# Transposing q by whole-array passes of the transpose mode for every unit of a fused attention and two-MLP kernel

## The chip, the cores and the metric

The kernel runs on one core of a Trainium2 chip. Its engines work side by side, each through an instruction list of its own, in order: PE (TensorE, matrix products, with a weight load ahead of each product), DVE (VectorE), ACT (ScalarE), POOL (GpSimd) and SP (SyncE, which here issues every DMA). The metric is the device time of one execution in microseconds; less is better.

## The reference, cut to what matters

```python
# q, k, v: (4, 8, 576, 64) float32, phi: (4, 8, 576, 32) float32
a = softmax(phi, axis=2)                        # over the 576 tokens
k_m = einsum('bhsm,bhsd->bhmd', a, k)           # 32 memory rows per head
v_m = einsum('bhsm,bhsd->bhmd', a, v)
attn = softmax(q @ k_m.T / 8)                   # over the 32 memories
x = (attn @ v_m).transpose(0, 2, 1, 3).reshape(2304, 512)
h = max(x @ w1, x @ w2, x @ w3)                 # 512 -> 768, weights in float64
x = h @ w_out                                   # 768 -> 512
g = softplus(x @ w_in)                          # 512 -> 2048
out = g @ w_out2                                # 2048 -> 512
```

## The kernel before, in words

**Units.** The attention is cut into eight units u = 0..7; a unit is one batch entry and four of its eight heads (u = 2 * batch + group). Units 0 to 3 are the first pair of batch entries, 4 to 7 the second pair. For a unit, phi, k and v are loaded, the softmax over tokens is made, and the compressed keys and values (32 memories of 4 heads stacked on 128 partitions, tile kvd) are transposed by small products with a 0/1 constant (L389 for values, and for the keys of units 0 to 3; L408 with another constant, `pick`, for the keys of units 4 to 7). att_q brings q to qT (head dimension on partitions, tokens along the row), att_sc multiplies it by the keys (L462 for units 0 to 3, L465 for 4 to 7), and the softmax over 32 memories follows as a chain over engines: att_sm0 (DVE: L474 transposes in 32x32 blocks, L477 takes the maximum), att_sm1 (POOL or DVE subtracts, L484; ACT takes the exponential, L485), att_sm2 (DVE sums, L491 to L493; POOL or DVE multiplies, L495), att_fin (DVE transposes back, L501; ACT rounds to the matrix format as ah, L506; al is what the rounding lost).

**q in two ways.** For units 0 to 3 (the set QPE), one DMA per unit brings 512 tokens of four heads, 4 neighbouring tokens of a head to a partition (1,024 bytes in a run), and a second one the last 64 tokens. PE multiplies each 128x64 block with the identity (L443, 16 blocks; L446, 4 blocks of 64 tokens), which leaves a head's transpose on half of the columns, and ACT's cast (L213) puts the tokens back into order with a strided write. For units 4 to 7 one DMA brings whole rows of 18 tokens (4,608 bytes), and DVE's transpose of 32x32 blocks (L452) makes all of qT in one instruction.

**MLP stages.** Values are multiplied into the weights first: u_mm (L565, and u_mr with L583 to L585 for the second pair) gives u = v w, in two parts uh and ul, and m1 multiplies u by attn (L611: ah by uh, al by uh, ah by ul, 18 matmuls for one block). m1out (L653 to L655) is the product with w_out, y0_split and L853, L885 are the second MLP. The float64 weights come as pairs of int32 (tile wraw) and are turned to float by ACT (L246), DVE and POOL. Four stages follow one another before the second MLP: phase_a(0) is m1 of the first pair, together with the keys and values of units 4 to 7; phase_o(0) is m1out of the first pair, and at slots from a table (`scs`) it takes up att_q, att_sc and the softmax of units 4 to 7; phase_a(1) is m1 of the second pair, which needs the ah of units 4 and 5, then that of 6 and 7; phase_o(1) ends the first MLP.

**What sets the order.** A list (PLAN) gives the program order of the first stages. From the program order a scheduler makes each engine's own order, and rotating buffers hold it back: products of units 4 to 7 share two PSUM tiles (pst), the others six (psm). q of units 4 to 7 has one buffer (tag qr), so that load_q(u + 1) is called after att_sc(u). SP issues all loads in its order, and each issue waits for the landing of the eighth one before it.

Of the kernel before, what the change touches and what calls it, by code (L numbers as in the profile page):

```python
# [117 lines left out]
C = {  # L118
    'load5': 5,
    'att': [[9, 9, 10, 11, 11], [10, 12, 12, 13, 13], [13, 13, 15, 15, 15], [15, 18, 19, 21, 21]],  # L120
    'wo': [[4, 5, 5], [6, 7, 7], [11, 11, 14], [11, 13, 17], [21, 22, 24], [23, 23, 23]],
    'scs': [[4, 4, 4, 4, 5, 6], [5, 5, 5, 6, 6, 7], [6, 6, 6, 7, 10, 10], [8, 11, 12, 13, 14, 18]],
    's1': ['pool', 'pool', 'pool', 'dve'],
    's2': ['dve', 'pool', 'pool', 'dve'],
    'al': ['pool', 'pool', 'pool', 'dve'],
    'u6': 7,
# [3 lines left out]
    'hl': ['dve'] + ['pool'] * 16 + ['dve'],  # L130
    'us0': 1,
    'us1': 0,
    'qpe': (0, 1, 2, 3),
}

@with_exitstack
def fused_kernel(ctx: ExitStack, tc: tile.TileContext, q, k, v, phi, w1, w2, w3, w_out, m_in, m_out, out):
# [7 lines left out]
    nc = tc.nc  # L145
    B, H, S, D = q.shape
# [3 lines left out]
    P = 128  # L150
# [28 lines left out]
    t_p = pool(a2_s, "a2", side="left")  # L179
# [18 lines left out]
    nc.vector.memset(onesq, 1.0)  # L198
    y1 = {}

    pick = const.tile([P, 4, P], F32, name="pick")
    pick2 = const.tile([P, 2, P], F32, name="pick2")
    nc.gpsimd.memset(pick, 0.0)
    nc.gpsimd.memset(pick2, 0.0)
    for h in range(4):
        a = slice(32 * h, 32 * h + 32)
        nc.vector.tensor_copy(pick[a, h, a], ident[a, a])
# [58 lines left out]
    units = [(b, g) for b in range(B) for g in range(NG)]  # L266
    U = defaultdict(dict)
    attn, vT = {}, {}
    QPE = C["qpe"]
    CK = {}  # L270

    def new_vT(pp):
# [34 lines left out]

    def load_q(u):
        b, g = units[u]
        if u in QPE:  # L310
            hs = slice(4 * g, 4 * g + 4)
            x = y1a_p.tile([P, 4, R4, D], F32, tag=f"ya{u}", name="qn")
            xr = wo_p.tile([SREM, 4, D], F32, tag=f"wol{2 + u}", name="qnr")
            dma(out=x.rearrange("p h r d -> p h (r d)"),
                in_=q[b, hs, 0:R4 * P, :].rearrange("h (p r) d -> p h (r d)", r=R4))
            dma(out=xr, in_=q[b, hs, R4 * P:S, :].rearrange("h p d -> p h d"))
            U[u]["qr"] = (x, xr)
            return
        if u < 4:
            qr = y1a_p.tile([P, NJB, 2, 32], F32, tag=f"ya{u}", name="qr")  # L320
        else:
            qr = t_p.tile([P, NJB, 2, 32], F32, tag="qr", name="qr")
        dma(out=qr.rearrange("p j a c -> p (j a c)"),
                          in_=q[b, 4 * g:4 * g + 4].rearrange("h (p j) d -> (h p) (j d)", j=NJB))
        U[u]["qr"] = qr

    def att_max(u):
        d = U[u]
# [52 lines left out]
    def att_tr(u, i):  # L381

        d = U[u]
        b, g = units[u]
        bl = b % 2
        st, kvd = d.pop(("xp", i)), d.pop(("kvd", i))
        if i or u in QPE:
            for s in range(2):
                nc.tensor.matmul(st[64 * s:64 * s + 64, P:2 * P], kvd, pick2[:, s], start=True, stop=True)  # L389
            if not i:  # L390
                kT = t_p.tile([P, 2, 64], F32, tag="kT", name="kT", bufs=4)
                nc.scalar.activation(out=kT, in_=st[:, P:2 * P].rearrange("p (a c) -> p a c", a=2), func=AF.Copy)
                d["kT"] = kT
                return
            CK["v", b, g] = 1
            sv = st[:, P:2 * P].rearrange("p (a c) -> p a c", a=2)
            if b < 2:
                nc.scalar.activation(out=vT[0][:, 2 * g:2 * g + 2, bl], in_=sv, func=AF.Copy)
                return
            vh, vl = vT[1]  # L400
            s0, sp = 4 * g + bl, 3 - 2 * bl
            nc.scalar.activation(out=vh[:, s0:s0 + sp + 1:sp, :], in_=sv, func=AF.Copy)
            nc.vector.tensor_tensor(out=vl[:, s0:s0 + sp + 1:sp, :], in0=sv, in1=vh[:, s0:s0 + sp + 1:sp, :],
                                    op=ALU.subtract)
            return
        for hf in range(2):
            for h in range(4):
                nc.tensor.matmul(st[32 * h:32 * h + 32, (1 + hf) * P:(2 + hf) * P], kvd[:, 32 * hf:32 * hf + 32],  # L408
                                 pick[:, h], start=True, stop=True)
        kT = t_p.tile([P, 2, 2, 64], F32, tag="kT", name="kT", bufs=4)  # L410
        sk = st[:, P:3 * P].rearrange("p (a s c) -> p a s c", a=2, s=2)
        if bl == 0:
            nc.scalar.activation(out=kT, in_=sk, func=AF.Copy)
        else:
            for s in range(2):
                nc.scalar.activation(out=kT[:, :, s], in_=sk[:, :, 1 - s], func=AF.Copy)
# [6 lines left out]
    def att_trs(u):  # L423
        att_tr(u, 1)
        att_tr(u, 0)

    def att_q(u, remeng="act"):
        d = U[u]
        qr = d.pop("qr")
        if u == 1:  # L430
            qT = h_p.tile([P, 2, S], F32, tag="h0", name="qT")
        elif u == 3:
            qT = y1a_p.tile([P, 2, S], F32, tag="ya0", name="qT")
        else:
            qT = t_p.tile([P, 2, S], F32, tag="qT", name="qT")
        if u in QPE:
            x, xr = qr
            rem = psm()
            for s in range(2):
                qp = psm()  # L440
                for r in range(R4):
                    for a in range(2):
                        nc.tensor.matmul(qp[64 * a:64 * a + 64, r * P:(r + 1) * P], x[:, 2 * s + a, r], ident,  # L443
                                         start=True, stop=True)
                for a in range(2):
                    nc.tensor.matmul(rem[64 * a:64 * a + 64, s * 64:s * 64 + 64], xr[:, 2 * s + a],  # L446
                                     ident[0:SREM, 0:SREM], start=True, stop=True)
                cast("act", qT[:, s, 0:R4 * P].rearrange("x (p r) -> x r p", r=R4), qp.rearrange("x (r p) -> x r p", r=R4))
            cast(remeng, qT[:, :, R4 * P:S], rem[:, 0:P].rearrange("p (s c) -> p s c", s=2))
            d["qT"] = qT  # L450
            return
        nc.vector.transpose(out=qT.rearrange("x a (p j) -> x a j p", j=NJB), in_=qr.rearrange("p j a c -> p a j c"))  # L452
        d["qT"] = qT

    def att_sc(u):
        d = U[u]
        kT, qT = d.pop("kT"), d.pop("qT")
        d["sc"] = []
        for c in range(2):
# [261 lines left out]
    def conv(i, p):  # L721
# [24 lines left out]
    for n in range(4):  # L746
        u = 4 + n
# [15 lines left out]
    for n in range(4):  # L763
        u = 4 + n
# [187 lines left out]
```

## Time and profile before

| what | value |
|---|---|
| median of 3 runs | 742.25 us (740.18 to 743.65) |
| the profiled execution | 739.94 us |
| its span in the trace | 738.1 us |
| its mean granted TensorE clock | 0.993 of full speed |
| PE busy | 703.9 us (95%) in 4808 instructions |
| DVE busy | 413.2 us (56%) |
| ACT busy | 297.6 us (40%) |
| POOL busy | 251.2 us (34%) |

The profiled execution lies 1.84 us above its span and 2.31 us below the median. PE is busy for 95% of the span, but not evenly: what it loses lies in the first 100 us and around 190 to 225 us, so that those stages are read by themselves.

### The profile page before, as it was taken

To read this page: it belongs to the slowest core of one execution; us is meant where nothing else is said; L and a number is where in the kernel's file an instruction comes from. 1 tells how busy PE (TensorE), PEld (TensorE's weight loads), DVE (VectorE), ACT (ScalarE), POOL (GpSimd) and SP (SyncE) were. 2 spreads that over 40 slices of the span, in tenths; PEclk is the share of its full clock that TensorE was granted. 3 is DMA by queue.
4 is the path that set the end of the run, shared out by engine and by line. 5 is a ranking of instruction groups with operands and counts; after the bars stand their busy time and mean duration, and the time that the engine had idled before them with its cause. 6 is when DMAs were issued, how large, how long until landed. Compare 5 with 4: busy or idle time off the path is not lost. (4 is left out here: it accounts for less than half of the span.)

```text
span 738.1 us, 12457 instructions
## 1 busy us (share of the span) xinstructions
PE 703.9 (95%) x4808; PEld 620.8 (84%) x4808; DVE 413.2 (56%) x788; ACT 297.6 (40%) x618; POOL 251.2 (34%) x240
## 2 busy tenths in 40 slices
PE   4979899999979999989999999999999999999997
PEld 3646777899869999978989889899888989889895
DVE  4479785426969974683332585333794335333342
ACT  2456464324567743653333453223442224222221
POOL 1012323114775414752222453222642224322221
PEclk9999999999999999999999999999999999999999
DMA  8997790201234201450000132000230000011112
GB/s 249 271 306 232 237 281 34 85 4 43 65 110 126 94 1 31 142 148 24 1 0 1 29 114 87 1 1 0 86 118 26 1 1 1 0 44 44 43 46 84
DMA packets 55195, 59.26 MB, mean 80 GB/s; under 512 B 10080, under 2 KB 49504, under 8 KB 55136
## 3 DMA queue, kind: packets, MB, share of 16 engines
q1 hardware_dynamic: 55136, 58.47, 26.4%
q8 instruction: 38, 0.62, 0.4%
q14 instruction: 21, 0.17, 0.1%
HBM read 53.74 MB, written 4.72 MB: 79 GB/s over the span
## 5 line engine op out<-in xcount | busy, mean ns | idle before, releaser
L221 POOL TENSOR_TENSOR gl<-m,gh 128x384 fp32r<-128x384 f32 x96 | 100.5, 1048 | 253.5 <-ACT gh L213 236.5
L859 DVE TENSOR_SCALAR e<-pst 128x384 int32<-128x384 int32 x96 | 53.1, 554 | 134.1 <-PE pst L853 134.0
L861 ACT ACTIVATE L<-e 128x384 f32<-128x384 f32 x96 | 50.3, 524 | 184.1 <-DVE e L859 184.1
L885 PE MATMUL acc<-oh,gh 128*128 128x512 f32 x288 | 113.7, 395 | 0.4 <-ACT gh L213 0.4
L885 PE MATMUL acc<-ol,gh 128*128 128x512 f32 x288 | 113.4, 394 | 0.0
L853 PE MATMUL pst<-yb,ih 128*128 128x384 f32 x384 | 102.1, 336 | 0.0
L611 PE MATMUL psm<-ah,uh 128*128 128x288 f32 x288 | 87.5, 308 | 3.7 <-ACT ya L213 2.5
L611 PE MATMUL psm<-ah,ul 128*128 128x288 f32 x288 | 85.5, 299 | 0.3 <-DVE ul L570 0.3
L611 PE MATMUL psm<-al,uh 128*128 128x288 f32 x288 | 85.7, 298 | 0.0
L863 DVE SCALAR_TENSOR_TENSOR m<-pst,L 128x384 f32<-128x384 f32 x96 | 53.3, 556 | 56.3 <-ACT L L861 54.2
L885 PE MATMUL acc<-oh,gl 128*128 128x512 f32 x288 | 82.7, 395 | 0.0
L213 ACT ACTIVATE gh<-m 128x384 fp32r<-128x384 f32 x96 | 50.0, 523 | 63.9 <-DVE m L863 61.2
L853 PEld LDWEIGHTS pst<-yb,ih 128*128 128x128 f32 x384 | 70.0, 188 | 3.4 <-DVE m L863 0.7
L853 PE MATMUL pst<-y0h,ih 128*128 128x384 f32 x192 | 64.8, 338 | 2.6 <-DVE m L863 2.5
L853 PE MATMUL pst<-y0l,ih 128*128 128x384 f32 x192 | 64.5, 336 | 0.0
L853 PE MATMUL pst<-y0h,il 128*128 128x384 f32 x192 | 64.5, 336 | 0.0
L853 PE MATMUL pst<-yb,il 128*128 128x384 f32 x192 | 64.4, 335 | 0.0
L885 PEld LDWEIGHTS acc<-oh,gl 128*128 128x128 f32 x288 | 53.6, 187 | 11.4
L611 PEld LDWEIGHTS psm<-ah,uh 128*128 128x128 f32 x288 | 54.4, 190 | 10.3 <-ACT ya L213 3.0
L885 PEld LDWEIGHTS acc<-oh,gh 128*128 128x128 f32 x288 | 53.9, 187 | 10.5 <-ACT gh L213 0.9
L885 PEld LDWEIGHTS acc<-ol,gh 128*128 128x128 f32 x288 | 54.0, 187 | 8.9
L611 PEld LDWEIGHTS psm<-al,uh 128*128 128x128 f32 x288 | 54.9, 191 | 0.4 <-issue 0.4
(147 smaller groups left out, 1342.0 us busy)
## 6 DMA issues: line engine op xcount, KB each, us to landing
wraw<-in_moe_w_dram SPq DMA_DIRECT2D x66, 256.0 KB, 4.4
raw<-in_moe_w_in_dram SPq DMA_DIRECT2D x16, 512.0 KB, 3.7
raw<-in_moe_w_out_dram SPq DMA_DIRECT2D x16, 512.0 KB, 3.6
out_dram<-o SPq DMA_DIRECT2D x18, 256.0 KB, 2.2
kvm<-in_v_dram SPq DMA_DIRECT2D x8, 512.0 KB, 7.4
kvm<-in_k_dram SPq DMA_DIRECT2D x8, 512.0 KB, 7.7
wor<-in_moe_w_out_dram SPq DMA_DIRECT2D x6, 512.0 KB, 5.9
qr<-in_q_dram SPq DMA_DIRECT2D x4, 576.0 KB, 4.7
```

The costliest lines, as they stand in the source:

```text
L213: nc.scalar.activation(out=dst, in_=src, func=AF.Copy)
L221: e.tensor_tensor(out=dst, in0=src, in1=hi, op=ALU.subtract)
L611: nc.tensor.matmul(x, l[:, t, ws], r[:, cs], start=(n == 0), stop=(n == 5))
L853: nc.tensor.matmul(hx, l[:, ds], r[:, cs], start=(n == 0), stop=(n == 3 * ND - 1))
L859: nc.vector.tensor_scalar(out=e.bitcast(I32), in0=hx.bitcast(I32), scalar1=0x7FFFFFFF, scalar2=None, op0=ALU.bitwise_and)
L861: nc.scalar.activation(out=L, in_=e, func=AF.Softplus, scale=-1.0)
L863: nc.vector.scalar_tensor_tensor(out=m, in0=hx, scalar=0.0, in1=L, op0=ALU.max, op1=ALU.add)
L885: nc.tensor.matmul(acc[0][t], l[:, t * P:(t + 1) * P], r, **kw)
```

## The change

q of all eight units takes one way. It is loaded with one DMA per head: token 128 r + p of a head goes to partition p, so that a run is one token's 64 numbers (256 bytes), and two heads lie side by side in the 128 columns of a block. Five DMAs take the place of two for each of units 0 to 3, and of one for each of units 4 to 7. PE transposes 128x128 blocks (two heads by 128 tokens) in the transpose mode over the whole array, 8 for a unit and 2 of 128x64 for the last tokens. The result has the tokens in order, so that ACT's cast reads and writes plain rows, two of 512 columns and one of 2 x 64. For units 4 to 7 the results go through the two pst tiles (ps = pst), where DVE's L452 touched no PSUM at all. The keys of units 4 to 7 take the constant of the others, two products instead of eight, and their scores are made as four products of 64 columns each, instead of four of 128 columns that accumulate in pairs. The constant `pick` goes. The softmax, the slots and all tables stay; line numbers after the edit are lower by 1 at the DMA helper and by 30 at m1.

```diff
     def load_q(u):
...
-            dma(out=x.rearrange("p h r d -> p h (r d)"),
-                in_=q[b, hs, 0:R4 * P, :].rearrange("h (p r) d -> p h (r d)", r=R4))
-            dma(out=xr, in_=q[b, hs, R4 * P:S, :].rearrange("h p d -> p h d"))
-            U[u]["qr"] = (x, xr)
-            return
...
-        dma(out=qr.rearrange("p j a c -> p (j a c)"),
-                          in_=q[b, 4 * g:4 * g + 4].rearrange("h (p j) d -> (h p) (j d)", j=NJB))
-        U[u]["qr"] = qr
+        for h in range(4):
+            dma(out=x[:, h // 2, :, (h % 2) * D:(h % 2 + 1) * D],
+                in_=q[b, 4 * g + h, 0:R4 * P, :].rearrange("(r p) d -> p r d", r=R4))
+        dma(out=xr, in_=q[b, hs, R4 * P:S, :].rearrange("h p d -> p h d"))
+        U[u]["qr"] = (x, xr)
...
-        if u in QPE:
-            x, xr = qr
-            rem = psm()
-            for s in range(2):
-                qp = psm()
-                for r in range(R4):
-                    for a in range(2):
-                        nc.tensor.matmul(qp[64 * a:64 * a + 64, r * P:(r + 1) * P], x[:, 2 * s + a, r], ident,
-                                         start=True, stop=True)
...
-                cast("act", qT[:, s, 0:R4 * P].rearrange("x (p r) -> x r p", r=R4), qp.rearrange("x (r p) -> x r p", r=R4))
...
-        nc.vector.transpose(out=qT.rearrange("x a (p j) -> x a j p", j=NJB), in_=qr.rearrange("p j a c -> p a j c"))
+        x, xr = qr
+        ps = psm if u < 4 else pst
+        for s in range(2):
+            qp = ps()
+            for r in range(R4):
+                nc.tensor.transpose(qp[:, r * P:(r + 1) * P], x[:, s, r], ident)
+            cast("act", qT[:, s, 0:R4 * P], qp)
+        rem = ps()
+        for s in range(2):
+            nc.tensor.transpose(rem[:, s * SREM:(s + 1) * SREM], xr[:, 2 * s:2 * s + 2].rearrange("p h d -> p (h d)"), ident[0:SREM, 0:SREM])
+        cast(remeng, qT[:, :, R4 * P:S], rem[:, 0:2 * SREM].rearrange("p (s c) -> p s c", s=2))
...
         for c in range(2):
             sc = pst() if u >= 4 else psm()
-            for s in range(2 if u in QPE else 0):
-                nc.tensor.matmul(sc[64 * s:64 * s + 64, 0:HS], kT[:, s], qT[:, s, c * HS:(c + 1) * HS],
+            for s in range(2):
+                nc.tensor.matmul(sc[64 * s:64 * s + 64, 0:HS], kT[:, s ^ flip], qT[:, s ^ flip, c * HS:(c + 1) * HS],
                                  start=True, stop=True)
-            for hf in range(0 if u in QPE else 2):
-                nc.tensor.matmul(sc[:, 0:HS], kT[:, hf].rearrange("p s c -> p (s c)"), qT[:, hf, c * HS:(c + 1) * HS],
-                                 start=(hf == 0), stop=(hf == 1))
```

On SP, before, this is the end of the loads of q for units 0 and 1 (qn holds 512 tokens, qnr the last 64):

```order
L184 DMA kvr<-in_k_dram 64x4x64
L184 DMA qn<-in_q_dram 128x4x256
L184 DMA qnr<-in_q_dram 64x4x64
L184 DMA qn<-in_q_dram 128x4x256
L184 DMA qnr<-in_q_dram 64x4x64
L184 DMA ph<-in_phi_dram 128x4x128
```

And after the change:

```order
L183 DMA kvr<-in_k_dram 64x4x64
L183 DMA qn<-in_q_dram 128x4x64 x4
L183 DMA qnr<-in_q_dram 64x4x64
L183 DMA qn<-in_q_dram 128x4x64 x4
L183 DMA qnr<-in_q_dram 64x4x64
L183 DMA ph<-in_phi_dram 128x4x128
```

Each load of qn has become four, and what follows them on SP (phi, values and keys of the next units, then the weights wraw of hidden block 1) stands three issues later for each unit.


On ACT, before, the stretch from the first conversion of the second weights, wraw of hidden block 1, to the first uh of m1 (L568):

```order
L246 ACTIVATE wh<-wraw 128x384
L246 ACTIVATE wl<-wraw 128x384
L506 ACTIVATE ah<-aT 128x576
L378 ACTIVATE kvd<-psm,ri 128x64
L485 ACTIVATE sT<-sT 128x576
L246 ACTIVATE wh<-wraw 128x384
L246 ACTIVATE wl<-wraw 128x384
L398 ACTIVATE v<-psm 128x2x64
L378 ACTIVATE kvd<-psm,ri 128x64 x3
L568 ACTIVATE uh<-psm 128x384 x3
```

And after the change, from the first conversion of the same weights on:

```order
L242 ACTIVATE wh<-wraw 128x384
L242 ACTIVATE wl<-wraw 128x384
L370 ACTIVATE kvd<-psm,ri 128x64
L538 ACTIVATE uh<-psm 128x384
L242 ACTIVATE wh<-wraw 128x384
L242 ACTIVATE wl<-wraw 128x384
L538 ACTIVATE uh<-psm 128x384 x3
L209 ACTIVATE qT<-psm 128x512
L384 ACTIVATE kT<-psm 128x128
L209 ACTIVATE qT<-psm 128x512
L209 ACTIVATE qT<-psm 128x2x64
```

The conversions of block 1 have moved behind the attn of units 0 and 1 (L476, L455) and behind most of the values and keys of units 2 and 3; behind the second pair of conversions there stand now three uh (L538) and the casts of unit 2's q.


On PE, before, unit 7's scores (L465) stand among the products of phase_o(0) (L653 to L655), with 72 of these still to come:

```order
L653 MATMUL psm<-hh,woh_2154 128x384
L654 MATMUL psm<-hh,wol_2155 128x384
L655 MATMUL psm<-hlo,woh_2154 128x384
L465 MATMUL pst<-qT,kT 128x288 x4
L653 MATMUL psm<-hh,woh_1160 128x384
L654 MATMUL psm<-hh,wol_1161 128x384
L655 MATMUL psm<-hlo,woh_1160 128x384
L653 MATMUL psm<-hh,woh_1274 128x384
L654 MATMUL psm<-hh,wol_1275 128x384
```

After the change, this is PE's order around unit 5's scores (L435) and the first blocks of m1 of the second pair (L581):

```order
L625 MATMUL psm<-hlo,woh_2094 128x384
L623 MATMUL psm<-hh,woh_2094 128x384
L435 MATMUL pst<-qT,kT 64x288 x4
L624 MATMUL psm<-hh,wol_2095 128x384
L625 MATMUL psm<-hlo,woh_2094 128x384
L623 MATMUL psm<-hh,woh_2094 128x384
L624 MATMUL psm<-hh,wol_2095 128x384
L625 MATMUL psm<-hlo,woh_2094 128x384
L581 MATMUL psm<-ah,uh 128x288 x3
L553 MATMUL psm<-wh,vh 128x384
L554 MATMUL psm<-wh,vl 128x384
```

Some 20 rows on, the transposes of unit 6's and unit 7's q (L419, and L423 for the last tokens; qr is the one buffer of q, filled anew between the two units) stand around unit 6's scores (L435):

```order
L581 MATMUL psm<-ah,uh 128x288
L581 MATMUL psm<-al,uh 128x288
L581 MATMUL psm<-ah,ul 128x288
L423 MATMUL pst<-ident,qr 128x64 x2
L435 MATMUL pst<-qT,kT 64x288 x4
L419 MATMUL pst<-ident,qr 128x128 x4
L581 MATMUL psm<-ah,uh 128x288 x4
L419 MATMUL pst<-ident,qr 128x128 x4
L423 MATMUL pst<-ident,qr 128x64 x2
```

And then unit 7's scores between blocks of m1:

```order
L581 MATMUL psm<-al,uh 128x288
L581 MATMUL psm<-ah,ul 128x288
L435 MATMUL pst<-qT,kT 64x288 x4
L581 MATMUL psm<-ah,uh 128x288
L581 MATMUL psm<-al,uh 128x288
L581 MATMUL psm<-ah,ul 128x288
L581 MATMUL psm<-ah,uh 128x288
L581 MATMUL psm<-al,uh 128x288
```

Unit 5's scores, which had 123 products of phase_o(0) behind them, now have five; unit 6's and 7's have moved out of phase_o(0) into phase_a(1). The four rows of L581 behind unit 7's first transposes are the first that need unit 5's ah. The first product that needs unit 7's ah (a row of L581) stands 24 matmuls behind unit 7's scores, and six of L553 to L555 are among these; on ACT four uh and eleven y0h stand between unit 7's ah and the next cast of m1 (mt).


## Rows read from the trace of the kernel before

**Rows 1.** Five stretches: us; busy PE, PEld, DVE, ACT, POOL; granted clock; DMA share; GB/s.

```profile
40.00:50.00 10.00, 6.90 (x116) 3.48 (x110) 6.88 (x20) 5.47 (x15) 0.77 (x2) 0.83 1.10 314
80.00:100.00 20.00, 17.56 (x241) 12.77 (x241) 15.91 (x44) 12.12 (x33) 5.32 (x7) 0.91 0.88 254
190.00:200.00 10.00, 8.66 (x47) 7.95 (x47) 9.97 (x18) 5.44 (x12) 6.92 (x6) 1.00 0.25 79
200.00:220.00 20.00, 16.88 (x93) 15.67 (x91) 14.39 (x23) 12.64 (x28) 13.91 (x13) 0.91 0.28 93
220.00:260.00 40.00, 37.53 (x263) 36.25 (x262) 37.10 (x79) 29.37 (x68) 20.74 (x20) 1.00 0.34 106
```

**Rows 2.** ACT in order of time: start us, us, instruction, then idle before and releaser.

```profile
45.76 0.55 ACT L246 ACTIVATE wh<-wraw 128x384 f32<-128x384 f32 x1 [1.30 <-DMA wraw<-in_moe_w_dram]
```

**Rows 3.** PE in order of time, first m1 and unit 3's transposes and scores.

```profile
56.54 0.40 PE L611 MATMUL psm<-ah,uh 128*128 128x288 f32 x1
...
60.74 1.10 PE L443 MATMUL psm<-ident,qn 128*64 128x128 f32 x16
...
62.44 1.76 PE L462 MATMUL psm<-qT,kT 128*64 128x288 f32 x8
```

**Rows 4.** PE and ACT in order of time around phase_o(0)'s end.

```profile
193.57 2.18 PE L465 MATMUL pst<-qT,kT 128*128 128x288 f32 x8 [1.34 <-DVE ssm L492]
...
215.45 0.40 PE L611 MATMUL psm<-ah,uh 128*128 128x288 f32 x1 [2.49 <-ACT ya L213]
...
209.63 0.69 ACT L506 ACTIVATE ah<-aT 128x576 fp32r<-128x576 f32 x1 [3.55 <-DVE aT L501]
...
211.19 3.83 ACT L213 ACTIVATE y0h<-ya 128x384 fp32r<-128x384 f32 x9 [0.50 <-issue]
```

**Rows 5.** DMA's queue in 24 to 26 us, then 40 to 42: packets, MB, share of 16 engines.

```profile
q1 hardware_dynamic: 904, 0.50, 112.8%
...
q1 hardware_dynamic: 725, 0.70, 109.7%
```

**Rows 6.** SP in order of time: the first issue of q, and the wraw of block 1.

```profile
15.55 0.60 SPq L184 DMA_DIRECT2D qn<-in_q_dram  x1
...
33.65 5.10 SPq L184 DMA_DIRECT2D wraw<-in_moe_w_dram  x6
```

**Rows 7.** Groups by line and shape: busy us, mean ns of one, idle before and releaser.

```profile
L336 PE MATMUL pst<-ident,mx 128*128 128x128 f32 x16 | 4.7, 383 | 5.7 <-DVE mx L334 5.7
L452 DVE STREAM_TRANSPOSE qT<-qr 128x1152 f32<-128x1152 f32 x4 | 9.2, 2307 | 0.0
```

**Rows 8.** PE in order of time: unit 6's key products.

```profile
165.94 0.64 PE L408 MATMUL pst<-pick,kvd 128*32 128x128 f32 x16
```

**Rows 9.** Groups by line and shape, the softmax chain of a unit.

```profile
L474 DVE STREAM_TRANSPOSE sT<-pst 128x288 f32<-128x288 f32 x8 | 3.7, 469 | 5.1 <-PE pst L465 5.1
L477 DVE TENSOR_REDUCE smx<-sT 128x18 f32<-128x576 f32 x8 | 5.8, 730 | 0.1
L484 POOL TENSOR_TENSOR sT<-sT,smx 128x576 f32<-128x576 f32 x7 | 8.1, 1160 | 25.9 <-DVE smx L477 25.9
L485 ACT ACTIVATE sT<-sT 128x576 f32<-128x576 f32 x8 | 5.4, 680 | 7.9 <-POOL sT L484 4.7 <-DVE sT L484 3.2
L491 DVE TENSOR_REDUCE ssm<-sT 128x18 f32<-128x576 f32 x8 | 5.8, 731 | 1.5 <-ACT sT L485 1.5
L495 POOL TENSOR_TENSOR sT<-sT,ssm 128x576 f32<-128x576 f32 x6 | 7.4, 1230 | 15.6 <-DVE ssm L493 15.5
L501 DVE STREAM_TRANSPOSE aT<-sT 128x576 f32<-128x576 f32 x8 | 6.1, 765 | 0.3 <-POOL sT L495 0.2
L506 ACT ACTIVATE ah<-aT 128x576 fp32r<-128x576 f32 x8 | 5.4, 680 | 6.6 <-DVE aT L501 6.6
```

**Rows 10.** The page's DMA issues, q of units 4 to 7: KB each, median us to landing.

```profile
qr<-in_q_dram SPq DMA_DIRECT2D x4, 576.0 KB, 4.7
```

More of the change, by code (lines that the diff above doesn't have):

```diff
@@ L132 @@
     'us1': 0,
-    'qpe': (0, 1, 2, 3),
 }
@@ L199, in fused_kernel @@
     y1 = {}
-    pick = const.tile([P, 4, P], F32, name="pick")
     pick2 = const.tile([P, 2, P], F32, name="pick2")
-    nc.gpsimd.memset(pick, 0.0)
     nc.gpsimd.memset(pick2, 0.0)
@@ L206, in fused_kernel @@
         a = slice(32 * h, 32 * h + 32)
-        nc.vector.tensor_copy(pick[a, h, a], ident[a, a])
         nc.vector.tensor_copy(pick2[a, h % 2, a], ident[a, a])
@@ L268, in fused_kernel @@
     attn, vT = {}, {}
-    QPE = C["qpe"]
     CK = {}
@@ L309, in load_q @@
         b, g = units[u]
-        if u in QPE:
-            hs = slice(4 * g, 4 * g + 4)
-            x = y1a_p.tile([P, 4, R4, D], F32, tag=f"ya{u}", name="qn")
+        hs = slice(4 * g, 4 * g + 4)
+        if u < 4:
+            x = y1a_p.tile([P, 2, R4, 2 * D], F32, tag=f"ya{u}", name="qn")
             xr = wo_p.tile([SREM, 4, D], F32, tag=f"wol{2 + u}", name="qnr")
-            dma(out=x.rearrange("p h r d -> p h (r d)"),
-                in_=q[b, hs, 0:R4 * P, :].rearrange("h (p r) d -> p h (r d)", r=R4))
-            dma(out=xr, in_=q[b, hs, R4 * P:S, :].rearrange("h p d -> p h d"))
-            U[u]["qr"] = (x, xr)
-            return
-        if u < 4:
-            qr = y1a_p.tile([P, NJB, 2, 32], F32, tag=f"ya{u}", name="qr")
-        else:
-            qr = t_p.tile([P, NJB, 2, 32], F32, tag="qr", name="qr")
-        dma(out=qr.rearrange("p j a c -> p (j a c)"),
-                          in_=q[b, 4 * g:4 * g + 4].rearrange("h (p j) d -> (h p) (j d)", j=NJB))
-        U[u]["qr"] = qr
+        else:
+            t = t_p.tile([P, R4 + 1, 4 * D], F32, tag="qr", name="qr")
+            x = t[:, 0:R4].rearrange("p h d -> p (h d)").rearrange("p (a r d) -> p a r d", a=2, r=R4)
+            xr = t[0:SREM, R4].rearrange("p (h d) -> p h d", h=4)
+        for h in range(4):
[3 more added lines that the diff above has]
+        U[u]["qr"] = (x, xr)
     def att_max(u):
@@ L386, in att_tr @@
         st, kvd = d.pop(("xp", i)), d.pop(("kvd", i))
-        if i or u in QPE:
-            for s in range(2):
[L389 to L404, printed above, removed]
-            return
@@ L406, in att_tr @@
[L406 to L416, printed above, removed]
@@ L417, in att_tr @@
-        d["kT"] = kT
+        for s in range(2):
+            nc.tensor.matmul(st[64 * s:64 * s + 64, P:2 * P], kvd, pick2[:, s], start=True, stop=True)
+        sv = st[:, P:2 * P].rearrange("p (a c) -> p a c", a=2)
+        if not i:
+            kT = t_p.tile([P, 2, 64], F32, tag="kT", name="kT", bufs=4)
+            nc.scalar.activation(out=kT, in_=sv, func=AF.Copy)
+            d["kT"] = kT
+            return
+        CK["v", b, g] = 1
+        if b < 2:
+            nc.scalar.activation(out=vT[0][:, 2 * g:2 * g + 2, bl], in_=sv, func=AF.Copy)
+            return
@@ L419, in att_kv @@
+        vh, vl = vT[1]
+        s0, sp = 4 * g + bl, 3 - 2 * bl
+        nc.scalar.activation(out=vh[:, s0:s0 + sp + 1:sp, :], in_=sv, func=AF.Copy)
+        nc.vector.tensor_tensor(out=vl[:, s0:s0 + sp + 1:sp, :], in0=sv, in1=vh[:, s0:s0 + sp + 1:sp, :],
+                                op=ALU.subtract)
     def att_kv(u):
@@ L435, in att_q @@
             qT = t_p.tile([P, 2, S], F32, tag="qT", name="qT")
-        if u in QPE:
-            x, xr = qr
-            rem = psm()
-            for s in range(2):
-                qp = psm()
-                for r in range(R4):
-                    for a in range(2):
-                        nc.tensor.matmul(qp[64 * a:64 * a + 64, r * P:(r + 1) * P], x[:, 2 * s + a, r], ident,
-                                         start=True, stop=True)
-                for a in range(2):
-                    nc.tensor.matmul(rem[64 * a:64 * a + 64, s * 64:s * 64 + 64], xr[:, 2 * s + a],
-                                     ident[0:SREM, 0:SREM], start=True, stop=True)
-                cast("act", qT[:, s, 0:R4 * P].rearrange("x (p r) -> x r p", r=R4), qp.rearrange("x (r p) -> x r p", r=R4))
-            cast(remeng, qT[:, :, R4 * P:S], rem[:, 0:P].rearrange("p (s c) -> p s c", s=2))
-            d["qT"] = qT
-            return
-        nc.vector.transpose(out=qT.rearrange("x a (p j) -> x a j p", j=NJB), in_=qr.rearrange("p j a c -> p a j c"))
+        x, xr = qr
[9 more added lines that the diff above has]
+        cast(remeng, qT[:, :, R4 * P:S], rem[:, 0:2 * SREM].rearrange("p (s c) -> p s c", s=2))
         d["qT"] = qT
@@ L457, in att_sc @@
         kT, qT = d.pop("kT"), d.pop("qT")
+        flip = units[u][0] % 2 if u >= 4 else 0
         d["sc"] = []
@@ L460, in att_sc @@
             sc = pst() if u >= 4 else psm()
-            for s in range(2 if u in QPE else 0):
-                nc.tensor.matmul(sc[64 * s:64 * s + 64, 0:HS], kT[:, s], qT[:, s, c * HS:(c + 1) * HS],
+            for s in range(2):
+                nc.tensor.matmul(sc[64 * s:64 * s + 64, 0:HS], kT[:, s ^ flip], qT[:, s ^ flip, c * HS:(c + 1) * HS],
                                  start=True, stop=True)
-            for hf in range(0 if u in QPE else 2):
-                nc.tensor.matmul(sc[:, 0:HS], kT[:, hf].rearrange("p s c -> p (s c)"), qT[:, hf, c * HS:(c + 1) * HS],
-                                 start=(hf == 0), stop=(hf == 1))
             d["sc"].append(sc)
```

## Prediction

> **What bounds the kernel now.** I read the page first: PE is busy 95% of the span and the chain that ended last runs on PE almost throughout, so what can move the end is PE work taken away or added, and holes in PE. The change touches only the first 220 us. The table of stretches shows how full PE is there [rows 1]: in 80 to 100 us it is busy 17.56 of 20 us at a granted clock of 0.91, in 200 to 220 us 16.88 of 20 at 0.91, while 220 to 260 us, with the same m1 products, is nearly full (37.53 of 40, 263 records, 0.143 us each). What an edit is worth is thus read from two places. The first is the start of m1: ACT in order of time stands still for the weights wraw of hidden block 1, whose last half lands only at 45.76 us [rows 2]; DMA shows a share above 1 in 40 to 50 us [rows 1], so that this landing is set by how much DMA time stands before it. The first m1 starts at 56.54 us [rows 3]. The second is the seam between phase_o(0) and phase_a(1): unit 7's scores start at 193.57 us, its ah is ready at 210.32 (209.63 + 0.69), and PE stands idle for 1.34 and 2.49 us around there [rows 4]. Summed over the seam, idle PE is 1.34 + 3.12 (200 to 220) + 2.47 (220 to 260) = 6.9 us, and the lower clock takes 0.09 x 20 = 1.8; together 8.7.
>
> **The change part by part.**
>
> *Loads of units 0 to 3.* The bytes stay, but a KB that was one packet is four of 256 bytes. The trace has no stretch with such packets alone, so I price them from two stretches in which the queue is saturated [rows 5]. In 24 to 26 us, 904 packets of about 560 bytes take 2 us x 16 x 1.128 / 904 = 39.9 ns each; in 40 to 42 us, 725 packets of 966 bytes take 48.4. A line through both is 28 ns a packet and 0.021 ns a byte: 33 ns at 256 bytes, 50 at 1,024. One unit's 512 KB then takes 2048 x 33 - 512 x 50 = 42 us more of engine time, over 16 engines at a share of 1.1 about 2.4 us. Bounds: 0, if a packet costs by its bytes; 4.3, if one of 256 bytes costs as much as one of 1,024. I take 2.4, since both stretches are mixtures whose mean size lies between the ends. The Trainium skill ("DMA: Bandwidth & Descriptors", section "Why small descriptors are slow (HBM only)") gives 11 cycles for 256 bytes, 3 of them overhead; by it a KB costs 44 cycles for 35, an estimate of 0.4 us a unit in place of 2.4. By that rule the start of m1 would come earlier, not later; no row here holds 256-byte packets by themselves, so it is one of the cases below.
>
> SP issues 12 more DMAs before that wraw; an issue takes 0.60 us, and from 15.55 to 33.65 us it made 18 of them, 1.0 us each [rows 6], so that it was mostly paced by landings; 12 x 0.6 = 7.2 us of issues fit beside 4 x 2.4 = 9.6 us of DMA time and add nothing (with cheap packets they would add at most about 1).
>
> *Start of m1.* wraw lands at 45.76 + 9.6 = 55.4 us. By the new order ACT then has eight rows ahead of the first m1: two conversions, three uh, three casts of unit 2's q. At 0.55 us, as in [rows 2], that is 4.4; unit 2's scores follow, half of the 1.76 in [rows 3]. m1 starts at 60.7 us, 4.2 later. Unit 3's transposes, which lie behind that start, become cheaper by 1.1: half a unit's 8 products took 1.10 us [rows 3], so 2.2 for 16, and the new 8 take 8 x 0.14 = 1.1. The price of a whole-array transpose is in no row: the lowest is a record of L443, 1.10 / 16 = 0.069 us (half the columns loaded), the highest the mean of L336, a single product with all the waiting in it, 0.383 us [rows 7]. I take 0.14, twice the low one, as 128 columns are loaded for 64. **+3.1 us** (-4 if packets cost by their bytes, +10.6 if 4.3; both under the rivals).
>
> *m1 of the first pair.* In 80 to 100 us PE loses 20 - 17.56 = 2.4 us idle and 1.8 by the clock [rows 1]. The keys and values of units 4 and 5 fill this stretch in one lump, and in the new order they come spread between m1 products; I take half of the 4.2 as regained (0 to 4.2): -2.1.
>
> *PE work of units 4 to 7.* Added: 8 x 0.14 + 0.15 for the rest = 1.27 us a unit, 5.1 in all. Removed: L408, 0.64 us a unit [rows 8] less 0.2 for the two products in their place, 1.8 in all; scores of 2.18 us [rows 4] become 1.76 as for units 0 to 3 [rows 3], 1.7 in all. Net +1.6, with -2.1 from above **-0.5 us**. DVE loses L452, 9.2 us [rows 7], which is off PE; ACT gains three casts a unit. Each unit needs three PSUM tiles of the two pst, so its last two products wait for a cast (about 0.55 us); m1 or m1out products stand between, else it would be up to 0.6 x 4 = 2.4 us.
>
> *The seam.* Here the order has moved most. Scores of units 5, 6 and 7 now stand at the very end of phase_o(0) and inside phase_a(1), so the softmax chain, which 72 products of m1out covered for unit 7, is covered by little. The bare chain, from scores to ah, is the sum of its rows [rows 9]: 2 x 0.47 + 0.73 + 1.16 + 0.68 + 0.73 + 1.23 + 0.77 + 0.68 = 6.9, with the two small operations on the sum about 7.2 us. Measured for unit 7 it was 210.32 - 195.75 = 14.6 us, with other work between on a DVE that was busy 19 of 20 us afterwards as well (37.10 of 40 in [rows 1]). I take 10.5, midway.
> From unit 5's scores to the first product that needs its ah, PE has 23 matmuls x 0.143, one and a half units of transposes (1.9) and unit 6's scores (1.76): 6.9 us. So it waits 3.6. A second wait lies inside the same stretch: qr has one buffer, so unit 7's q is loaded only after unit 6's transposes, and its own stand right behind unit 6's scores. A load of q takes 4.7 us to land [rows 10] against 1.76 of scores, so PE stands about 2.9, and all of m1 behind it. The two waits overlap (2.9 of the 3.6).
> From unit 7's scores to the product that needs its ah there are 24 x 0.143 = 3.4 us: a wait of 7.1. On ACT four uh and eleven y0h stand ahead of the next mt, 15 x 0.41 us (3.83 for 9 in [rows 4]) = 6.2, of which PE's free PSUM tiles cover another 24 products: 2.8 more. The clock, 1.8 before with 6.9 us idle, I put at 2.5 with 13.5 idle. Sum 3.6 + 7.1 + 2.8 + 2.5 = 16.0 against 8.7: **+7.3 us** (-2 to +12).
>
> **Sum.** 739.94 + 3.1 - 0.5 + 7.3 = 749.8 us, said as 750. The profiled execution lies 2.3 us below the median; I don't add this.
>
> **The rivals.**
> - *A, as above*: 750, own range 745 to 757.
> - *B, the softmax chain runs bare* (not slower): DVE is freed of 9.2 us, and the chain at the seam takes its 7.2 us. Then the load of unit 7's q alone stops PE (2.9), unit 7's wait is 3.8, y0h is covered by PSUM and the clock stays up: 6.7 for 8.7, in all 739.94 + 3.1 - 0.5 - 2.0 = 740.5. For it: every row of the chain in the trace is short. Against: DVE is over 90% busy behind the seam, and two chains now overlap. Below a chain of about 8 us this case decides.
> - *C, cheap 256-byte packets*: wraw still lands at 45.76, which by ACT's rows puts m1 at 51.1; with SP's issues about 1 later that is 52.5, or 4 us earlier than before (unit 3's 1.1 set against unit 2's later keys) instead of 3.1 later. The rest as in A: 742.7. This is the case of the Trainium skill's rule above. For it: a record of the DMA shows only mixed sizes. Against: the line through the two windows.
> - *B and C together*: 733.4, the only case clearly faster.
> - *D, dear packets*, 4.3 us a unit: m1 starts at 68, +10.6 for +3.1: 757.
> - *E, the transposes aren't single passes*, 0.38 us each as L336 shows: 8 x 0.24 x 4 = 7.7 us more: 757. The Trainium skill ("TensorE: Matmul & The Clock Gate", "Part 4: PE-mode transpose") tells of about 275 ns in one kernel, by which units 4 to 7 would take 4.3 us more than my sum. No row here shows a transpose.
>
> **How the numbers follow.** A 0.48, B 0.20, C 0.14, B and C 0.08, D 0.06, E 0.04. The bound of 0.5%, 3.7 us, is about what a measurement can tell from no change. Faster comes from B and C together and a third of B and C each, 0.20; same from the rest of B and C, 0.21 with little of A, 0.22; slower 0.58. The likeliest is A, 750. B with C lies below 737, as does a fifth of B; above 758 stands half of D and E, so 737 to 758 leaves out just under two in ten.
>
> **What would show it.** Right: wraw's second half read by ACT near 55 us and the first m1 near 60; L419 at about 0.14 us a record or pair; holes of PE near unit 7's transposes (released by DMA of qr), ahead of unit 5's ah and, the largest, of unit 7's ah; a granted clock below 1 there. Wrong: a start of m1 before 56 us, which takes the packets out; a seam with under 8 us of idle PE, which takes the chain out; records of L419 at 0.3 us or more.

## The result, and the profile after

The changed kernel takes 748.46 us, median of 4 runs (747.0 to 748.97); the kernel before took 742.54 in the runs beside it. The ratio is 1.0089, with a 95% interval of 1.0065 to 1.0113: slower by about 6 us. The profiled execution of the changed kernel took 748.15 us with a span of 746.3, against 739.94 and 738.1 before: 8.2 us more.

Where it lies is read first from DVE in order of time, at the last write of h in either half of m1 (line L619 before, L589 after; start, us, instruction, idle before). This is the kernel before, at the end of m1 of the first pair of batch entries and at the end of m1 of the second pair:

```profile
156.16 0.45 DVE L619 TENSOR_TENSOR h<-mt,psm 128x288 f32<-128x288 f32 x1
...
285.74 0.45 DVE L619 TENSOR_TENSOR h<-mt,psm 128x288 f32<-128x288 f32 x1 [0.28 <-PE psm L611]
```

And the same two places after the change:

```profile
153.75 0.45 DVE L589 TENSOR_TENSOR h<-mt,psm 128x288 f32<-128x288 f32 x1 [0.28 <-PE psm L581]
...
293.71 0.46 DVE L589 TENSOR_TENSOR h<-mt,psm 128x288 f32<-128x288 f32 x1 [0.28 <-PE psm L581]
```

The changed kernel is 2.4 us ahead when the first half ends and 8.0 behind when the second does: all of the loss, 10.4 us, arises between them, and nothing more comes behind. The stretch between the two ends, before and after, with the columns of [rows 1]:

```profile
156.61:286.19 129.58, 122.59 (x892) 116.67 (x891) 94.98 (x179) 70.00 (x157) 59.39 (x54) 0.99 0.20 63
...
154.20:294.17 139.97, 128.98 (x934) 119.38 (x933) 93.54 (x180) 77.11 (x171) 60.47 (x54) 0.95 0.22 62
```

Idle PE grew by 4.0 us there (10.99 for 6.99) and busy PE by 6.4, with 42 more records at a lower mean clock. So the 10.4 us are not waiting alone: a part is the low clock, and a part is work: the transposes that DVE made before, and what has moved over from the first half (922 records of PE from the first m1 to that half's end, for 1,001). The table of stretches for the changed kernel (the last two lines are parts of the one above them) shows where:

```profile
40.00:50.00 10.00, 8.59 (x76) 4.08 (x72) 1.91 (x5) 3.13 (x9) 0.00 (x0) 0.67 0.85 243
80.00:100.00 20.00, 19.28 (x191) 15.23 (x188) 18.82 (x48) 11.73 (x31) 4.02 (x6) 1.00 0.86 269
190.00:200.00 10.00, 10.00 (x60) 9.00 (x60) 5.43 (x11) 3.73 (x7) 2.41 (x2) 1.00 0.40 112
200.00:220.00 20.00, 16.31 (x107) 12.60 (x105) 16.04 (x27) 11.19 (x25) 10.10 (x9) 1.00 0.35 88
220.00:260.00 40.00, 32.70 (x199) 30.67 (x200) 34.44 (x65) 28.20 (x64) 24.52 (x23) 0.83 0.35 108
...
220.00:240.00 20.00, 13.18 (x60) 11.38 (x60) 15.61 (x26) 13.45 (x31) 13.88 (x13) 0.66 0.30 95
...
225.00:230.00 5.00, 3.35 (x10) 2.36 (x10) 3.51 (x7) 2.20 (x5) 0.00 (x0) 0.50 0.61 172
```

Against [rows 1], 80 to 100 us is now full (19.28 for 17.56), and 220 to 260 us, which was nearly full (37.53 of 40), has 7.3 us of idle PE, almost all of it in 220 to 240, at a granted clock of 0.66. PE in order of time names the waits (start, us, instruction, idle before and what ended it):

```profile
209.41 0.71 PE L435 MATMUL pst<-qT,kT 128*64 128x288 f32 x4 [1.18 <-DVE sT L444]
211.01 0.66 PE L419 MATMUL pst<-ident,qr 128*128 128x128 f32 x4 [0.89 <-DMA qr<-in_q_dram]
...
214.35 1.19 PE L435 MATMUL pst<-qT,kT 128*64 128x288 f32 x8
...
222.63 0.85 PE L581 MATMUL psm<-ah,uh 128*128 128x288 f32 x2 [4.25 <-ACT ah L476]
224.91 0.61 PE L581 MATMUL psm<-al,uh 128*128 128x288 f32 x1 [1.43 <-POOL al L217]
...
225.55 0.44 PE L581 MATMUL psm<-al,uh 128*128 128x288 f32 x1
225.79 0.44 PE L581 MATMUL psm<-ah,ul 128*128 128x288 f32 x1
227.59 0.85 PE L581 MATMUL psm<-ah,uh 128*128 128x288 f32 x2 [1.35 <-ACT ah L476]
```

The rows at 222.63 and 227.59 are the first products that need the ah of unit 6 and of unit 7. Unit 7's scores end at 215.54, its ah is ready 12.0 us later. Products of 288 columns follow one another in 0.24 us here (225.55 to 225.79), for 0.13 in a full stretch: the granted clock from 225 to 230 us is 0.50, the lower of the two levels (1.2 GHz), after PE had stood still for 4.25 us. DVE in order of time shows why the chain is not bare. Its rows between unit 7's scores and ah:

```profile
216.56 0.47 DVE L444 STREAM_TRANSPOSE sT<-pst 128x288 f32<-128x288 f32 x1
...
217.37 0.74 DVE L447 TENSOR_REDUCE smx<-sT 128x18 f32<-128x576 f32 x1
...
218.56 1.38 DVE L454 TENSOR_TENSOR sT<-sT,smx 128x576 f32<-128x576 f32 x1
...
221.09 0.77 DVE L471 STREAM_TRANSPOSE aT<-sT 128x576 f32<-128x576 f32 x1
...
222.36 0.74 DVE L461 TENSOR_REDUCE ssm<-sT 128x18 f32<-128x576 f32 x1
...
223.69 1.57 DVE L246 SCALAR_TENSOR_TENSOR cg<-wraw,cg 128x384 int32<-128x384 int32 x1
225.19 0.74 DVE L465 TENSOR_TENSOR sT<-sT,ssm 128x576 f32<-128x576 f32 x1
226.04 0.78 DVE L471 STREAM_TRANSPOSE aT<-sT 128x576 f32<-128x576 f32 x1
```

The transpose at 221.09 is unit 6's, and at 223.69 a weight conversion that m1 will need only later stands for 1.57 us between unit 7's sum and its product.

### The profile page after: what moved, and what is told of

It is laid out like the page before. It is cut to its first block, busy times and chain, and to the rows that moved or that the text cites. A ratio compares the mean times of both kernels' runs of the same rounds, so it can differ in the third digit from the quotient of the medians.

```text
span 746.3 us, 12243 instructions
## 1 busy us (share of the span) xinstructions
PE 706.1 (95%) x4680; PEld 619.9 (83%) x4680; DVE 412.1 (55%) x780; ACT 299.0 (40%) x628; POOL 252.1 (34%) x239
## 5 line engine op out<-in xcount | busy, mean ns | idle before, releaser
L581 PE MATMUL psm<-ah,uh 128*128 128x288 f32 x288 | 88.7, 315 | 8.6 <-ACT ah L476 5.9
L581 PE MATMUL psm<-al,uh 128*128 128x288 f32 x288 | 86.8, 303 | 1.4 <-POOL al L217 1.4
L581 PE MATMUL psm<-ah,ul 128*128 128x288 f32 x288 | 85.9, 302 | 0.0
L581 PEld LDWEIGHTS psm<-ah,uh 128*128 128x128 f32 x288 | 55.1, 194 | 16.3 <-ACT ah L476 7.0
L855 PEld LDWEIGHTS acc<-oh,gh 128*128 128x128 f32 x288 | 53.9, 187 | 10.5 <-ACT gh L209 0.9
L581 PEld LDWEIGHTS psm<-al,uh 128*128 128x128 f32 x288 | 56.0, 195 | 2.2 <-POOL al L217 1.8
```

Source lines behind the costliest of these rows:

```text
L581: nc.tensor.matmul(x, l[:, t, ws], r[:, cs], start=(n == 0), stop=(n == 5))
L855: nc.tensor.matmul(acc[0][t], l[:, t * P:(t + 1) * P], r, **kw)
```

## The experiments

Three theories stood after the result. S: the loss is the seam's, because the transposes of units 4 to 7 take turns on the two pst tiles and so push scores to the end of phase_o(0). L: it is the loads', because 12 more DMAs hold up the start of m1. P: it is PE's own work on transposes, and the clock. Ratios are to runs of the kernel before on the same chip, with a 95% interval.

**The change for units 0 to 3 only.** Load and att_q of units 4 to 7, L408 and L465 stay.

```diff
         if u in QPE:
...
-            dma(out=x.rearrange("p h r d -> p h (r d)"),
-                in_=q[b, hs, 0:R4 * P, :].rearrange("h (p r) d -> p h (r d)", r=R4))
+            for h in range(4):
+                dma(out=x[:, h // 2, :, (h % 2) * D:(h % 2 + 1) * D],
+                    in_=q[b, 4 * g + h, 0:R4 * P, :].rearrange("(r p) d -> p r d", r=R4))
...
-                        nc.tensor.matmul(qp[64 * a:64 * a + 64, r * P:(r + 1) * P], x[:, 2 * s + a, r], ident,
-                                         start=True, stop=True)
+                    nc.tensor.transpose(qp[:, r * P:(r + 1) * P], x[:, s, r], ident)
+                cast("act", qT[:, s, 0:R4 * P], qp)
...
```

> Units 0 to 3 take the changed way (loads by head, whole-array transposes), units 4 to 7 stay as before. Theory S (the time is lost at the seam, since the transposes of units 4 to 7 take turns on the two pst tiles and push the scores of units 5 to 7 to the end of phase_o(0)): the seam is as before, m1 of the first pair ends some 2 us earlier, 740.5 us (738 to 742.5). Theory L (12 more DMAs ahead of the weights of block 1 hold up m1): 745 to 749, as after the change. Theory P (PE work of the transposes and the clock are the cost): 742 to 744.

740.16 us, ratio 0.9997 (0.9974 to 1.002): no change. m1 of the first pair ends at 155.02 and that of the second at 284.75, 129.7 us apart; in the kernel before it was 129.6. The seam is as it was, and the 12 DMAs with what comes beside them lose nothing net, which speaks against L.

**The change for units 4 to 7 only.** The reverse: the changed kernel, with the old load and the old products for units 0 to 3.

```diff
+        if u < 4:
+            x, xr = qr
...
+                        nc.tensor.matmul(qp[64 * a:64 * a + 64, r * P:(r + 1) * P], x[:, 2 * s + a, r], ident,
+                                         start=True, stop=True)
...
         x, xr = qr
-        ps = psm if u < 4 else pst
+        ps = pst
```

> Units 4 to 7 take the changed way, units 0 to 3 stay as before. Theory S: the whole loss is here, 750.5 us (748 to 753), with 10 to 14 us of idle PE from 200 to 250 us and the largest hole ahead of unit 7's ah. Theory L: 742 to 744. Theory P: 744 to 746, without the holes.

749.61 us, ratio 1.0104 (1.0082 to 1.0126): all of the loss. PE, in order of time, at the largest hole:

```profile
228.87 0.85 PE L602 MATMUL psm<-ah,uh 128*128 128x288 f32 x2 [7.92 <-ACT ah L497]
```

The hole stands ahead of the first product that needs unit 7's ah. S holds, and P falls as far as it says that the work itself costs this: one hole of 7.92 us is most of the loss. Two things are less neat than S has them: idle PE from 200 to 250 us is 9.8 us, just under the 10 to 14 expected, and of the 8.6 us by which the second half of m1 ends later (294.35 for 285.74), 2.4 stand already at the end of the first half (158.58 for 156.16).

**Transposes of units 4 to 7 through psm.**

```diff
-        ps = psm if u < 4 else pst
+        ps = psm
```

> The changed kernel, but the transposes of units 4 to 7 go through the six psm tiles instead of the two pst tiles; nothing else. The order then has unit 7's scores with 41 products of phase_o(0) still to come. Theory S: most of the seam's loss comes back, 742 us (740 to 745), idle PE at the seam under 8 us, and the wait for unit 7's ah under 3. A rival to it, that the transposes now take psm tiles from the four sums of m1out and hold these up: 746 to 750, with PE idle inside phase_o(0). Theories L and P: 748, unchanged.

744.77 us, ratio 1.0052 (1.0031 to 1.0072). Against 1.0089, some 3 of the 6 us come back. The time lies just within the range that S gave, above its likeliest 742, and the wait for ah is gone from PE's list of waits. In its place stand 4.9 us of waits for the last u of the next blocks (ul, two waits) and 1.1 us for the DMA of qr. Idle PE from 180 to 260 us is 5.6 us, less than before (6.9). So pst's turns are shown to set the place of the scores, and the place of the scores to cost the wait for ah; what remained was open.

**Four loads of 1 KB runs.** The kernel before, with q of units 0 to 3 loaded by head, nothing else.

```diff
-            dma(out=x.rearrange("p h r d -> p h (r d)"),
-                in_=q[b, hs, 0:R4 * P, :].rearrange("h (p r) d -> p h (r d)", r=R4))
+            for h in range(4):
+                dma(out=x[:, h].rearrange("p r d -> p (r d)"),
+                    in_=q[b, 4 * g + h, 0:R4 * P, :].rearrange("(p r) d -> p (r d)", r=R4))
```

> The kernel before, with q of units 0 to 3 loaded by one DMA per head but still in runs of 1,024 bytes. If the number of DMAs delays the weights of block 1 (each issue waits for the landing of the eighth before it): the second half of wraw is read by ACT 3 to 5 us later than 45.76, at 49 to 51 us. If the size of the packets did it: at 45 to 47 us. Time: within 3 us of before in either case.

wraw's second half is read at 49.23 us, 3.5 later than [rows 2]; in the changed kernel it was 50.59, 4.8 later. So most of the delay is the number of DMAs, not the size of the packets. The one execution took 749.42 us, 8 above the median of before beside it, where 3 was the most expected. In its trace the first m1 starts at 61.80 us, 5.3 later than before, and the first half of m1 ends at 166.92, 10.8 later. That is more than the delay of the weights, and a single execution doesn't tell what the rest is.

**Loads in 256-byte runs with the old products.** This parts loads and casts from the transposes.

```diff
-            dma(out=x.rearrange("p h r d -> p h (r d)"),
-                in_=q[b, hs, 0:R4 * P, :].rearrange("h (p r) d -> p h (r d)", r=R4))
+            for h in range(4):
+                dma(out=x[:, h], in_=q[b, 4 * g + h, 0:R4 * P, :].rearrange("(r p) d -> p r d", r=R4))
...
-                cast("act", qT[:, s, 0:R4 * P].rearrange("x (p r) -> x r p", r=R4), qp.rearrange("x (r p) -> x r p", r=R4))
+                cast("act", qT[:, s, 0:R4 * P], qp)
```

> The kernel before, but q of units 0 to 3 loaded by head in runs of 256 bytes, and ACT's cast of qT plain; the 64-column products of the transposes stay. It parts the loads and casts from the products: if the whole-array transposes are what gives back the loads' cost in first_pair_only, it is at 744 to 750, as with four_loads_1kb; if the plain casts do, at 740 to 743.

748.23 us, ratio 1.0094 (1.0068 to 1.0121). The loads by head, with the order that comes of them, cost some 7 us, the plain casts don't make up for it, and the whole-array transposes give back as much in the change for units 0 to 3 only. The cost does not lie ahead of m1. PE's first row of m1 and DVE's last write of h in the first half, in order of time:

```profile
56.53 0.61 PE L611 MATMUL psm<-ah,uh 128*128 128x288 f32 x1
...
162.97 0.45 DVE L619 TENSOR_TENSOR h<-mt,psm 128x288 f32<-128x288 f32 x1 [0.28 <-PE psm L611]
```

m1 starts as in the kernel before (56.54), though wraw's second half is read only at 51.96 us, and its first half ends 6.8 us later (162.97 for 156.16). Between the two PE is idle for 4.8 us (2.8 before), at a mean clock of 0.96 (0.98 before), with as many records (1,003 for 1,001). Which of the waits there is the loads' was not isolated. The group of the 64-column products here, then that of the whole-array transposes with units 0 to 3 changed (both of the whole span):

```profile
L443 PE MATMUL psm<-ident,qn 128*64 128x128 f32 x128 | 12.7, 319 | 0.5 <-DVE ul L570 0.5
```

```profile
L442 PE MATMUL psm<-ident,qn 128*128 128x128 f32 x32 | 5.9, 336 | 3.1 <-ACT kT L393 2.8 <-DVE ul L568 0.3
```

128 records for 64 products have become 32 for 32 transposes, 6.8 us of PE less, ahead of and within m1 of the first pair. (In the kernel before the group of L443 was 11.3 us, so against that it is 5.4.)

**Later loads.** In the change for units 0 to 3 only, q of units 2 and 3 is loaded after the weights of block 1.

```diff
-    ('q', 2),
-    ('q', 3),
...
     ('wl', 1, 1),
+    ('q', 2),
+    ('q', 3),
```

> first_pair_only (units 0 to 3 changed, units 4 to 7 as before), with q of units 2 and 3 loaded after the weights of block 1 instead of ahead of them. If the 12 further DMA issues are what holds up m1, wraw's second half is read by ACT at 42 to 46 us, 6 to 10 earlier than the 52.09 of first_pair_only, the first m1 starts at 51 to 55 us, and the time falls to 736 (733 to 739), below the kernel before. If unit 2's late q then holds up the softmax of units 2 and 3 in its place: 739 to 743.

737.02 us, ratio 0.995 (0.9932 to 0.9968): faster than both kernels. ACT reads wraw's second half at 43.59 us, 8.5 earlier than without this edit, and the first m1 starts at 53.91 (58.46 without). Little of that start is left at the end of the first half of m1, 154.40 us for 155.02, so the gain of 3 us can't be read from the start of m1.

**The same edit in the kernel before.**

```diff
-    ('q', 2),
-    ('q', 3),
...
     ('wl', 1, 1),
+    ('q', 2),
+    ('q', 3),
```

> The kernel before, with q of units 2 and 3 loaded after the weights of block 1, and nothing else. It parts first_pair_q_late's gain. If the later loads alone give it (their place on SP), it lies 3 to 5 us below before, 736 to 738. If the gain is the whole-array transposes', freed of what their 12 more DMAs cost, it lies within 2 us of before: 739 to 743.

741.52 us, ratio 1.0001 (0.9986 to 1.0016). Two rows of it, ACT's and PE's in order of time:

```profile
41.44 0.55 ACT L246 ACTIVATE wh<-wraw 128x384 f32<-128x384 f32 x1 [1.40 <-DMA wraw<-in_moe_w_dram]
```

```profile
56.28 0.40 PE L611 MATMUL psm<-ah,uh 128*128 128x288 f32 x1
```

The weights come 4.3 us earlier than in [rows 2], and m1 starts 0.26 earlier than in [rows 3]. So in the kernel before the weights did not set the start of m1, and the later loads by themselves gain nothing. The 0.5% of the run ahead belongs to the change of units 0 to 3, and in it, by the loads in 256-byte runs, to the whole-array transposes, once their DMAs are out of the way.

**Two buffers for q of units 4 to 7, in the changed kernel.**

```diff
-            t = t_p.tile([P, R4 + 1, 4 * D], F32, tag="qr", name="qr")
+            t = t_p.tile([P, R4 + 1, 4 * D], F32, tag="qr" if u % 2 == 0 else "qrb", name="qr")
```

> The changed kernel with two buffers for q of units 4 to 7, so that unit 7's load does not wait for unit 6's transposes; the transposes still go through pst. If the load's wait is a part of the loss (2.9 us in the prediction): 744.5 to 746.5. If pst's turns set the order, as theory S says: 747.5 to 748.5 and the wait for the DMA of qr (0.89 us) gone without a gain.

746.82 us, ratio 1.0075 (1.0051 to 1.0099). This lies between the two ranges. The DMA's wait is gone and the wait for ah (4.22 us in one) stays, as S has it; 1 us may have been gained, which lies within the interval of the changed kernel's own ratio.

**psm and later loads, then with two buffers as well.** The three edits together are what the changed method can be mended to.

```diff
-    ('q', 2),
-    ('q', 3),
...
     ('wl', 1, 1),
+    ('q', 2),
+    ('q', 3),
...
-        ps = psm if u < 4 else pst
+        ps = psm
...
+            t = t_p.tile([P, R4 + 1, 4 * D], F32, tag="qr" if u % 2 == 0 else "qrb", name="qr")
```

> transposes_in_psm with the same later loads of units 2 and 3. If loads and seam are two separate costs, it falls by as much as first_pair_q_late does against first_pair_only: 741 (738 to 743). If the two are one, nothing: 745.

744.44 us, ratio 1.0044 (1.0029 to 1.006). The loads' edit gives nothing here in the end: the first half of m1 ends 3.0 us earlier (149.50 for 152.48), but the stretch between the two ends becomes 2.6 us longer, and in it PE now waits 2.4 us for the DMA of qr (1.1 without the edit).

> psm_q_late with two buffers for q of units 4 to 7. In psm_q_late PE waits 2.4 us once for the load of q behind unit 4's transposes. If that wait is what is left of the second pair's cost once the scores stand early: 741.5 to 742.5, the wait gone. If the rest is the lower place of unit 7's softmax and u of the second pair, as the waits of L581 for ul suggest: 743.5 to 745.

741.47 us, ratio 0.999 (0.9974 to 1.0007). That wait is gone and 3 us with it: all units changed, and no slower than before. The seam is not mended by that: between the two ends of m1 lie 135.8 us, 6.2 more than before, and the first half ends 5.6 earlier (150.57 for 156.16), which makes up for it. It still stands behind the version with only units 0 to 3 changed (0.995), and PE's largest wait is 4.6 us, for ul; whether that wait is the rest wasn't tried.

## Why the prediction was right, point by point

**The sign and the size.** 750 was forecast, 748.46 was measured, and the bulk of it by the forecast mechanism: case A. The sum was 739.94 + 3.1 - 0.5 + 7.3. Parted at the end of the first half of m1, with the 1.6 us of work on units 4 to 7 counted to the second part, +1.0 and +8.9 were forecast, and -2.4 and +10.4 came. The two parts were off by 3.4 and 1.5 us in opposite directions, so that the nearness of the total is in part luck.

**The seam** (+7.3 forecast, 16.0 for 8.7). Idle PE from 180 to 260 us is 11.0 us after and 6.9 before. At the clock 0.34 x 20 = 6.8 are lost after, against 1.8; 17.8 for 8.7, by the forecast's own count. (Idle time at the low clock is counted twice in that, before and after.) By its terms: the waits for unit 6's and unit 7's ah and al are 4.25 + 1.43 + 1.35 = 7.0, for 7.1 forecast; the chain took 12.0 us for 10.5, so the right sum has a part of luck, since unit 6's ah, which the sum left out, was the first to be late. The wait for unit 5 was forecast at 3.6 with the load's 2.9 within it, and was 0.89 for the load and none for ah, whose chain took 8.8 us (202.73 to 211.54). The scores of unit 6 waited 1.18 us more, in the middle, which the sum doesn't have. The y0h casts were put at 2.8 and cost at most 1.5: they ran from 230.33 to 234.97 us, and behind them PE waited for mt for 1.13 and 0.35 us, with weight conversions on DVE in between. The clock was put at 2.5 and took 6.8 by that count, the term that was mis-sized most. What it cost PE's work is less: from 222 to 234 us the granted clock was 0.50 and PE busy for 8.2 us, of which half, some 4 us, is the clock's (an estimate).

**The cause of the new order.** The prediction read the new places from the order, without saying why they came. Transposes in psm and the change for units 4 to 7 only show it: three pst uses more for each unit, in turns on two tiles, whereas DVE's transpose needed none. With psm, unit 7's scores stand ahead of 41 products of phase_o(0), and no wait for ah is left at the seam.

**The start of m1** (+4.2 forecast, 57.40 us after, so +0.9). Here the step failed in two ways. First, the price: packets of 256 bytes were to take 33 ns. The window from 22 to 24 us of the changed kernel holds nothing else (packets, MB, share of 16 engines):

```profile
q1 hardware_dynamic: 1022, 0.25, 57.4%
```

2 us x 16 x 0.574 / 1022 = 18 ns each, below the line through two mixed windows. The queue wasn't full there, but from 24 to 26 us, at a share of 86.2%, 1,579 packets took as long, 17.5 ns. By 18 ns a unit's 512 KB take 2048 x 18 - 512 x 50 = 11 us of engine time more, 0.7 us over 16 engines, not 2.4. The Trainium skill's rule ("DMA: Bandwidth & Descriptors", "Why small descriptors are slow (HBM only)"), 44 cycles for 35 per KB or, as an estimate, 0.4 us a unit, lies closer than my line did. But its case C, an early m1, did not come, since the packets' time wasn't what set the landing: the share is 57%, and SP made the issues one behind another. SP in order of time in the changed kernel, the loads of units 0 and 2 and the weights:

```profile
15.11 5.15 SPq L183 DMA_DIRECT2D qn<-in_q_dram  x4
...
32.39 5.40 SPq L183 DMA_DIRECT2D qn<-in_q_dram  x4
...
42.95 3.12 SPq L183 DMA_DIRECT2D wraw<-in_moe_w_dram  x6
```

The first wraw of block 1 is issued at 42.95, 9.3 us later than in [rows 6], and ACT reads its second half 4.8 later. The 20 issues of q ahead of it took 0.51 to 1.76 us each, 19.2 together; before, 8 issues took 7.6. None of these was held by the landing of the eighth issue before it: that lay 0.37 us back or more when each began. So the issues of q were not "paced by landings", and "12 x 0.6 us of issues fit beside the DMA time and add nothing" was wrong: the issues were most of the delay, as four loads of 1 KB runs show with 3.5 us and no small packet. (There the 20 issues took 12.1 us, and several began within 0.02 us of that landing; why an issue takes 0.5 us or 1.8 was not tried.) Second, the bound: the start of m1 does not hang on wraw in the kernel before, as the later loads there show, and the loads in 256-byte runs cost 7 us without moving it. What stood in the way there was, by the whole-array transposes' effect, PE's work ahead of and within the first half of m1; that PE and not the chain behind it was the reason is argued, not shown.

**The transposes** (0.14 us each forecast, single passes). PE in order of time at full clock:

```profile
61.12 1.03 PE L419 MATMUL psm<-ident,qn 128*128 128x128 f32 x8
```

0.13 us each, one record a transpose. Case E is out. So is the estimate worked out from the 275 ns of the Trainium skill's "TensorE: Matmul & The Clock Gate" ("Part 4: PE-mode transpose") as the time between two transposes; as the time of one record (274 ns is the mean of the 32 of units 4 to 7) it agrees. Of the gain, the prediction counted only unit 3's 1.1 us, as if PE's other transposes were covered; loads in 256-byte runs with and without them differ by some 7 us.

**m1 of the first pair** (half of 4.2 regained). PE lost 0.7 us in 80 to 100 us, with the clock at 1.00, so 3.5 were regained.

## What to carry to other kernels

Count the uses of a small rotating pool before moving work into it: three more PSUM tiles a unit, in two that others wait for, moved the scores out of the work that covered their chain. The change for those units cost 1% (1.0104), and six tiles in place of two gave back some 0.4% in the changed kernel (1.0052 for 1.0089). Where one engine issues all DMAs, one behind another, an issue that brings a quarter of the bytes still took 0.51 to 1.76 us here, so a load split in four delays what stands behind it even when its packets are cheap; put what is needed first ahead of it. A wait that shows in the trace is a bound only if what stands behind it moves when it goes: bring it forward alone, once, before building a sum on it.

## What the runs showed of the hardware that had not been expected

- A DMA packet of 256 bytes took 18 ns where the queue held nothing else (1,022 in 2 us at a share of 57.4%; 17.5 ns at 86.2%), well below the 28 ns that two mixed windows gave as the fixed part alone.
- Four DMAs in place of one, with the same runs of 1 KB, delayed the weights behind them by 3.5 us. With runs of 256 bytes the 20 issues of q took 19.2 us of SP, with runs of 1 KB 12.1.
- In 220 to 240 us of the changed kernel the granted clock was 0.66, with PE busy 13.18 of 20 us: after a hole of 4.25 us, products of 288 columns came at 0.24 us each, for 0.13 in a full stretch, and the clock stayed at 0.50 until 234 us.
